# First expert's weight loads tied to all seven routing phases instead of the first one

## The chip, the cores and the metric

The kernel runs on one core of a Trainium2 chip. The metric is the time of one execution on the device, in microseconds (us); lower is better. Five engines work side by side, each through its own list of instructions in order: TensorE (PE: matmuls, and transposes done as matmuls), VectorE (DVE), ScalarE (ACT), GpSimd (POOL) and SyncE (SP, which issues nearly all DMA transfers here).

## What is computed

Three stages, each fed by the one before. Attention over 4 batches of 12 heads (448 tokens, head size 64) with normalised queries and keys; an MLP with an ELU (768 to 2048 to 768) on the 1792 tokens that come out; and a mixture of 8 experts (768 to 1024 to 768) to which the tokens are dealt greedily, at most 224 to an expert:

```python
def _moe_ref(x, w_in, w_out):
    h = x @ w_in
    g = np.where(h > 0.0, h, alpha * (np.exp(np.minimum(h, 0.0)) - 1.0))
    return g @ w_out

def _moe2_ref(x, w_gate, w1, w2):
    cap = N // E
    flat = (x @ w_gate).flatten()
    for idx in np.argsort(-flat):
        tok, e = idx // E, idx % E
        if assigned[tok] >= 0 or counts[e] >= cap:
            continue
        assigned[tok] = e
        counts[e] += 1
    for e in range(E):
        mask = assigned == e
        out[mask] = np.maximum(x[mask] @ w1[e], 0.0) @ w2[e]
```

Matrix products are made of three float16 products each (high part times high, low times high, high times low), so every weight is split on the chip into two float16 tiles.

## The kernel before

**Order of the work.** Up to about 610 us the kernel does attention and the first product of the MLP. From there to about 890 us PE does the MLP's second product (tile `py`, function `second`) and, in between, the routing that deals tokens to experts. After that come the eight experts (`expert`), each with its weights loaded by `load_expert` and its tokens gathered by `gather`. One caller weaves the two: `route_units` gives a number at each `yield` of `Route.phase`, and the loop around it puts as many `py` matmuls into PE's list as that number is worth. So the routing has PE's gaps filled by a fixed list of `py` work, and PE's order is written out by hand.

**A routing phase.** There are seven (`Route.phase(i)`, i = 0 to 6; this text counts them in the same way) and a `finish`. A phase finds each open token's best expert (L91 to L99 on DVE), transposes the scores (PE, `rt_pb`), copies them to `rt_row` (L117), makes 14 comparison tiles `rt_C` on DVE (L127) whose sums PE takes into `rt_pc`, copies these (L138 on ACT, L139 on DVE into `rt_cs`), transposes them on PE (`rt_pg`), and then goes through a chain of small steps that passes between DVE and PE: L151, L152, L154 on DVE, `rt_pm` on PE, L158, `rt_pt` on PE, L162 to L213, `rt_pp` on PE, L175 to L182, `rt_pc` (of `rt_sc`) on PE, L186 to L193, and the next phase's L91. Each PE step of this chain stands in PE's list behind `py` matmuls, and the `py` matmuls behind it wait for it.

`self.marks.append(i)` (L135) notes the last `rt_C` comparison of each phase, so that seven marks exist.

**Loading an expert.** An expert has 14 weight chunks: six of W1 (128 x 1024 float32, 512 KB) and eight of W2 (128 x 768, 384 KB). For each, `load_steps` issues one DMA from SP into a staging tile `st` (L362; three staging buffers, so the fourth load waits until the first chunk is split), and `split` makes the high part on ACT (L350) and the low part on DVE (L351):

```python
st = stg.tile([P, w], F32, tag="st", name="st")
i = nc.sync.dma_start(st, src)
if hold:
    tc.add_manual_dep(i.ins, hold[-1].ins.name, NOSYNC, reason="not before its turn")
split(hi, lo, st, w)
```

`hold[-1]` is what a load is tied to. The tie is of the kind NOSYNC: a scheduler, which places every instruction in the list of its engine by simulated times, may not place the load earlier than the mark. No semaphore comes of it; on the chip SP issues the load when the instructions ahead of it on SP are done and its staging buffer is free. `load_expert(0)` appends the mark of phase 0 to `hold`, and that stays the last entry for all experts.

**Tiles.** Expert 0's weights go to the buffers of pool `wuA`, which are free once the MLP's first product is done (about 611 us). Expert 1's go to `wuB`, which holds `w_out` until the last `py` matmuls. SP also issues the loads of the MLP's middle values (`g`, L790 and L794) and the stores of finished rows `xh` (L817, made by L815 on ACT and L816 on DVE) that the gathers of the experts read.

Of the kernel before, what the change touches and what calls it, by code (L numbers as in the profile page):

```python
# [255 lines left out]
def kernel(  # L256
# [25 lines left out]
    KC = DM // P  # L282
    NF = FF // P
    NF1 = F1 // P
# [61 lines left out]
    hold = []  # L346
# [6 lines left out]
    def load_split(hi, lo, src):  # L353
        for _ in load_steps(hi, lo, src):
            pass

    def load_steps(hi, lo, src):

        w = src.shape[1]
        if src.dtype == F32:  # L360
# [5 lines that stand above are left out]
            yield  # L366
            return

        for a in range(0, w, 512):
            n = min(512, w - a)  # L370
            st = stg.tile([P, n, 2], I32, tag="st", name="st")
            nc.sync.dma_start(st.rearrange("p n t -> p (n t)"), src[:, a:a + n].bitcast(I32))
            cv = gat.tile([P, n], I32, tag="cv", bufs=3, name="cv")
            i = DVE.tensor_scalar(cv, st[:, :, 1], 3, 0x3FFFFFF8, op0=ALU.logical_shift_left, op1=ALU.bitwise_and)
            if pace:
                tc.add_manual_dep(i.ins, pace[-1].ins.name, NOSYNC, reason="not before its turn")
            DVE.scalar_tensor_tensor(cv, st[:, :, 1], -0x40000000, cv, op0=ALU.bitwise_and, op1=ALU.bitwise_or)  # L377
            DVE.scalar_tensor_tensor(cv, st[:, :, 0], 29, cv, op0=ALU.logical_shift_right, op1=ALU.bitwise_or)
            cf = cv.bitcast(F32)
            ACT.activation(cf, cf, AF.Copy, scale=SW)  # L380
            ACT.copy(hi[:, a:a + n], cf)
            POOL.tensor_sub(lo[:, a:a + n], cf, hi[:, a:a + n])
            yield
# [475 lines left out]
    R = Route(nc, mmo, rconst, rsb, psR, dram, NCH, NE, CAP, B, S, id32, id16)  # L859
# [29 lines left out]
    ex = ctx.enter_context(tc.tile_pool(name="ex", bufs=2))  # L889
    KH = KC // 2  # L890

    def load_expert(e):
        if e == 0:
            hold.append(R.marks[0])
        pool = wuB if e % 2 else wuA
        W1 = pool.tile([P, 2, KC, F1], F16, tag="wu", name=f"w1_{e}")
        W2 = pool.tile([P, 2, NF1, DM], F16, tag="wu", name=f"w2_{e}")
        for c in range(KC):
            load_split(W1[:, 0, c, :], W1[:, 1, c, :], w1[e, c * P:(c + 1) * P, :])
        for c in range(NF1):  # L900
            load_split(W2[:, 0, c, :], W2[:, 1, c, :], w2[e, c * P:(c + 1) * P, :])
        return W1, W2

# [18 lines left out]
    def expert(e, W1, W2, xT):  # L922
# [33 lines left out]
        for hh in range(2):  # L956
# [15 lines left out]
            stores.append(st)  # L972

    W, xT = load_expert(0), gather(0)
    for e in range(NE):
        W_, x_ = W, xT
        if e + 1 < NE:
            W, xT = load_expert(e + 1), gather(e + 1)
        expert(e, *W_, x_)
# [30 lines left out]
```

## Time and profile before

| | |
|---|---|
| median of 3 runs | 1160.86 us (1159.09 to 1165.01) |
| the profiled execution | 1164.11 us, its span 1162.4 us |
| PE busy | 1039.3 us, 89% of the span |
| DVE busy | 784.2 us, 67% |
| ACT busy | 539.2 us, 46% |
| mean granted PE clock | 0.963 |

The span runs from the first to the last instruction; the execution's own time is 1.7 us longer. "Busy" is time in which an engine executes; idle time costs only where the chain that ends last goes through it. A timeline row gives start, duration, engine, line, operation and operands, how many instructions were merged into it, and in brackets how long the engine sat idle before it and what ended that. "xN" behind a busy time is a count of instructions.

### The profile page before, as it was taken

The numbers are of one execution on the slowest core, as the hardware profiler recorded it, in microseconds if no ns is written. First come the engines' busy times: TensorE is split into PE (matmuls) and PEld (weight loads), VectorE is DVE, ScalarE is ACT, GpSimd is POOL, SyncE is SP. The second block draws the span as 40 slices with busy tenths as digits, with TensorE's granted clock in tenths as the row PEclk, the third lists the DMA queues.
The fourth block names the chain that finished last, engine by engine and source line by source line (L and its number), as shares of the span: only waits on it lengthen the run. The fifth ranks groups of instructions, "written<-read, shape, count | busy, mean of one in ns | idle before, by whom it ended". The sixth has DMA issues, their size and how long they took to land.

```text
span 1162.4 us, 19353 instructions
## 1 busy us (share of the span) xinstructions
PE 1039.3 (89%) x7030; PEld 608.4 (52%) x7030; DVE 784.2 (67%) x1567; ACT 539.2 (46%) x1099; POOL 353.9 (30%) x462
## 2 busy tenths in 40 slices
PE   0687879897989999999999699999999898999997
PEld 0233334343444445444444345555546687888885
DVE  3788898999988775554337777877775565556520
ACT  2676677776777664554430410011102455555520
POOL 3687775757746451220000000000000412222100
PEclk9888889998999989999999899999999899999999
DMA  6355575569997825336823641030003778778710
GB/s 172 78 133 132 147 207 151 145 178 255 245 256 195 194 68 121 81 95 225 328 55 113 194 167 50 21 130 21 22 21 101 239 236 263 223 244 258 237 47 24
DMA packets 190319, 176.48 MB, mean 152 GB/s; under 512 B 114704, under 2 KB 161808, under 8 KB 189456
## 3 DMA queue, kind: packets, MB, share of 16 engines
q1 hardware_dynamic: 186064, 163.78, 49.5%
q0 software_dynamic: 3328, 11.01, 3.0%
q8 instruction: 55, 0.90, 0.3%
q10 hardware_dynamic: 832, 0.46, 0.1%
q14 instruction: 40, 0.33, 0.1%
HBM read 125.92 MB, written 31.98 MB: 136 GB/s over the span
## 4 chain that ended last, share of the span: by engine, by line
PE 48%; DVE 16%; DMA 13%; issue 10%; ACT 6%; POOL 4%; SPq 2%; POOLq 0%; DVEq 0%; ACTq 0%
PE py L324 17%; PE ph L324 12%; DMA st<-in_moe_w_dram 7%; PE po L324 4%; PE pye L324 3%; PE phe L324 3%; PE ps L324 3%; PE rt_pc L324 2%; DVE w L351 2%; DVE sm L533 2%; ACT w L350 2%; DVE cv L377 2%; PE pta L324 2%; DMA qn<-in_q_dram 2%; PE pl L324 1%
## 5 line engine op out<-in xcount | busy, mean ns | idle before, releaser
L324 PE MATMUL ph<-xT,w_in 128*128 128x448 f16 x1152 | 246.1, 358 | 8.2 <-DVE elu_g L685 5.2
L324 PE MATMUL py<-w_out,g 128*128 128x384 f16 x1152 | 204.5, 329 | 0.0
L324 PEld LDWEIGHTS <-w_in 128*128 128x128 f16 x1152 | 107.7, 99 | 127.7 <-issue 46.1
L351 DVE SCALAR_TENSOR_TENSOR w<-st,w 128x768 f16<-128x768 f32 (+1 forms) x112 | 119.2, 1072 | 76.7 <-ACT w L350 71.5
L545 POOL TENSOR_SCALAR pe<-pe,sm 128x448 f32<-128x448 f32 x168 | 126.7, 764 | 138.8 <-DVE sm L541 70.3
L324 PEld LDWEIGHTS <-g 128*128 128x128 f16 x1152 | 107.4, 98 | 89.3 <-issue 26.7
L324 PE MATMUL ps<-kT,qT 64*128 64x448 f16 (+1 forms) x576 | 97.0, 392 | 56.2 <-ACT pe L535 30.7
L350 ACT ACTIVATE w<-st 128x768 f16<-128x768 f32 (+1 forms) x112 | 103.6, 933 | 90.8 <-DMA st<-in_moe_w_dram 86.5
L535 ACT ACTIVATE pe<-ps,sm 128x448 f32<-128x448 f32 x168 | 105.9, 634 | 50.0 <-DVE sm L533 47.4
L324 PE MATMUL pye<-w,hT 128*112 128x512 f16 (+1 forms) x768 | 126.4, 326 | 0.0
L324 PEld LDWEIGHTS <-w 128*128 128x128 f16 x1152 | 111.8, 100 | 3.3 <-DVE xTe L917 1.2
L127 DVE TENSOR_SCALAR rt_C<-rt_row,rt_m 128x1792 f16<-128x1792 f32 x98 | 107.2, 1149 | 8.2 <-PE rt_pc L324 7.4
L324 PE MATMUL phe<-xTe,w 128*128 128x224 f16 x1080 | 111.4, 264 | 1.1 <-DVE xTe L917 1.1
L533 DVE TENSOR_REDUCE sm<-ps 128x1 f32<-128x448 f32 x168 | 100.2, 615 | 17.2 <-PE ps L324 15.2
L324 PEld LDWEIGHTS <-hT 128*112 128x112 f16 x768 | 91.6, 130 | 32.2
L815 ACT ACTIVATE xh<-py 128x384 f16<-128x384 f32 x28 | 13.7, 491 | 175.0 <-PE py L324 158.1
L324 PEld LDWEIGHTS <-qT 64*128 64x128 f16 (+1 forms) x576 | 27.7, 102 | 99.9 <-issue 66.7
L324 PE MATMUL pta<-id,pe 128*128 128x128 f32 x384 | 64.4, 289 | 15.1 <-POOL pe L545 5.8
L967 POOL DMA_INDIRECT out_dram<-yo,idx x16 | 19.5, 1220 | 179.6 <-DVE yo L966 178.0
L685 DVE SCALAR_TENSOR_TENSOR elu_g<-ph,elu_e 128x448 f32<-128x448 f32 x64 | 39.6, 619 | 48.3 <-ACT elu_e L683 48.1
L324 PEld LDWEIGHTS pta<-id,pe 128*128 128x128 f32 x384 | 45.2, 146 | 44.3 <-POOL pe L545 14.7
L201 POOL MEMSET rt_c<- 128x8 f16 x8 | 0.9, 123 | 220.7 <-DVE rt_c L207 216.6
(176 smaller groups left out, 1470.0 us busy)
## 6 DMA issues: line engine op xcount, KB each, us to landing
st<-in_moe_w_dram SPq DMA_DIRECT2D x48, 512.0 KB
st<-in_moe_w_dram SPq DMA_DIRECT2D x64, 384.0 KB
st<-in_moe_w_in_dram SPq DMA_DIRECT2D x24, 512.0 KB
g_d<-gt SPq DMA_DIRECT2D x64, 192.0 KB
g<-g_d SPq DMA_DIRECT2D x16, 768.0 KB
st<-in_moe_w_out_dram SPq DMA_DIRECT2D x16, 512.0 KB
gl<-g_d SPq DMA_DIRECT2D x32, 192.0 KB
wo_d<-wo SPq DMA_DIRECT2D x16, 384.0 KB
```

The source lines that it names most:

```text
L127: i = DVE.tensor_scalar(C.rearrange("p c t -> p (c t)"), row, m[:, s:s + 1], None, op0=ALU.is_le)
L201: nc.gpsimd.memset(c[:, 0:1, :], 0.0)
L324: i = PE_mm(o, l, r, **kw)
L350: ACT.activation(hi, st, AF.Copy, scale=SW)
L351: DVE.scalar_tensor_tensor(lo, st, SW, hi, op0=ALU.mult, op1=ALU.subtract)
L377: DVE.scalar_tensor_tensor(cv, st[:, :, 1], -0x40000000, cv, op0=ALU.bitwise_and, op1=ALU.bitwise_or)
L533: i = DVE.tensor_reduce(out=st[:, 0, u:u + 1], in_=ps[u], axis=AX.X, op=ALU.max, negate=True)
L535: ACT.activation(p[:, u, :], ps[u], AF.Exp, bias=st[:, 0, u:u + 1], accum_out=st[:, 1, u:u + 1])
L545: POOL.tensor_scalar(p[:, u, :], p[:, u, :], st[:, 2, u:u + 1], 1.0, op0=ALU.mult, op1=ALU.mult)
L685: DVE.scalar_tensor_tensor(gf, ph, -SG / SH, e, op0=ALU.mult, op1=ALU.min)
L815: ACT.activation(xh[:, 0], py, AF.Copy, scale=-SX2 / (SG * SW))
L967: st = POOL.indirect_dma_start(out=out, out_offset=bass.IndirectOffsetOnAxis(ap=idx[:, 1, 2 * e + hh:2 * e + hh + 1], axis=0), in_=yo, in_ ...
```

## The change

`load_expert` no longer appends one mark ahead of all loads. A small function `pace_first` appends, for expert 0 alone, a mark before each chunk: chunk c (0 to 13) gets mark number c * 7 // 14, so chunks 0 and 1 are tied to phase 0, chunks 2 and 3 to phase 1, and so on to chunks 12 and 13 in phase 6. The last entry of `hold`, to which the loads of the other experts are tied, is then the mark of phase 6 instead of phase 0.

```diff
+    def pace_first(e, c):
+
+        if e == 0:
+            hold.append(R.marks[c * len(R.marks) // (KC + NF1)])
+
     def load_expert(e):
-        if e == 0:
-            hold.append(R.marks[0])
         pool = wuB if e % 2 else wuA
         W1 = pool.tile([P, 2, KC, F1], F16, tag="wu", name=f"w1_{e}")
         W2 = pool.tile([P, 2, NF1, DM], F16, tag="wu", name=f"w2_{e}")
         for c in range(KC):
+            pace_first(e, c)
             load_split(W1[:, 0, c, :], W1[:, 1, c, :], w1[e, c * P:(c + 1) * P, :])
         for c in range(NF1):
+            pace_first(e, KC + c)
             load_split(W2[:, 0, c, :], W2[:, 1, c, :], w2[e, c * P:(c + 1) * P, :])
```

The lists of PE and POOL keep their order. On DVE, ACT and SP the splits and loads of expert 0 move. In DVE's list, here the part of phase 0 behind its last `rt_C` (a difference; `w_0_9673` is expert 0's W1, `w_0_9674` its W2):

```order
 L351 SCALAR_TENSOR_TENSOR w_0_9673<-st,w_0_9673 128x1024
 L151 TENSOR_TENSOR rt_w<-rt_pg,rt_rc 128x112
-L351 SCALAR_TENSOR_TENSOR w_0_9673<-st,w_0_9673 128x1024
 L152 SCALAR_TENSOR_TENSOR rt_w<-rt_w,rt_m 128x112
 L154 TENSOR_REDUCE rt_t_7162<-rt_w 128x1
-L351 SCALAR_TENSOR_TENSOR w_0_9673<-st,w_0_9673 128x1024
 L158 TENSOR_REDUCE rt_t_7162<-rt_pm 1x1
-L351 SCALAR_TENSOR_TENSOR w_0_9673<-st,w_0_9673 128x1024
 L162 COPY rt_t_7162<-rt_pt 128x1
 L166 TENSOR_SCALAR rt_ab<-rt_m,rt_t_7162 128x14
 L168 TENSOR_SCALAR rt_at<-rt_m,rt_t_7162 128x14
-L351 SCALAR_TENSOR_TENSOR w_0_9673<-st,w_0_9673 128x1024
```

Of 14 splits that stood between the steps of phase 0's chain, two stay in phase 0, both ahead of L151; the other twelve are gone from it. In DVE's list of phase 1, the part behind its `rt_C` (a difference):

```order
 L816 SCALAR_TENSOR_TENSOR xh<-py,xh 128x384
 L127 TENSOR_SCALAR rt_C<-rt_row,rt_m 128x1792
+L351 SCALAR_TENSOR_TENSOR w_0_9673<-st,w_0_9673 128x1024
 L139 CAST rt_cs<-rt_pc 64x128
 L151 TENSOR_TENSOR rt_w<-rt_pg,rt_rc 128x112
+L351 SCALAR_TENSOR_TENSOR w_0_9673<-st,w_0_9673 128x1024
 L152 SCALAR_TENSOR_TENSOR rt_w<-rt_w,rt_m 128x112
 L154 TENSOR_REDUCE rt_t_7519<-rt_w 128x1
```

Phase 1 has got two splits, one ahead of L139 and one between L151 and L152. In phases 2 to 6 the first stands ahead of L139 too, and the second between L139 and L151; in ACT's list the two L350 of a phase stand on either side of L138. SP's list as it is with the change, from the stores at the start of phase 0 to phase 2 (`st` a staging tile, `x2_d` the finished rows, `g2` and `gt2` the MLP's middle values):

```order
L817 DMA x2_d0_82<-xh_6908 128x768
L362 DMA st_9675<-in_moe2_w1_dram 128x1024
L362 DMA st_9679<-in_moe2_w1_dram 128x1024
L817 DMA x2_d1_83<-xh_7008 128x768
L817 DMA x2_d0_82<-xh_7109 128x768
L790 DMA g2_7535<-g_d2_78 128x3072 x4
L817 DMA x2_d1_83<-xh_7194 128x768
L362 DMA st_9683<-in_moe2_w1_dram 128x1024
L817 DMA x2_d0_82<-xh_7337 128x768
L362 DMA st_9687<-in_moe2_w1_dram 128x1024
L794 DMA gt2_7540<-gt_d1_81 128x4096
L817 DMA x2_d1_83<-xh_7438 128x768
```

Before, all 14 loads of expert 0 and the first three of expert 1 stood ahead of the `g2` load. Now two do, and chunks 2 and 3 stand behind it, each behind a store of `xh`.

## Rows read from the trace of the kernel before

**Rows 1.** Windows: busy time (count) of PE, PEld, DVE, ACT, POOL; clock, DMA share, GB/s.

```profile
621.73:669.46 47.73, 36.21 (x243) 18.84 (x240) 37.81 (x67) 15.77 (x20) 0.13 (x1) 0.93 0.51 162
669.46:703.79 34.33, 33.54 (x240) 18.32 (x241) 26.23 (x60) 3.13 (x6) 0.13 (x1) 1.00 0.44 162
...
644.60:669.46 24.86, 13.90 (x74) 7.28 (x71) 18.52 (x47) 10.68 (x13) 0.13 (x1) 0.86 0.75 231
692.68:703.79 11.11, 11.11 (x72) 6.62 (x71) 7.81 (x37) 0.49 (x1) 0.13 (x1) 1.00 0.35 112
```

**Rows 2.** Timeline of PE in phase 0.

```profile
661.04 0.25 PE L324 MATMUL rt_pp<-rt_c,rt_one 128*128 128x112 f16 x1 [6.61 <-DVE rt_c L213]
661.09 4.04 PE L324 MATMUL py<-w_out,g 128*128 128x384 f16 x12
```

**Rows 3.** Timeline of DVE in phase 0.

```profile
644.07 1.23 DVE L351 SCALAR_TENSOR_TENSOR w<-st,w 128x1024 f16<-128x1024 f32 x1
...
656.20 0.96 DVE L351 SCALAR_TENSOR_TENSOR w<-st,w 128x768 f16<-128x768 f32 x1 [0.81 <-ACT w L350]
...
660.78 0.21 DVE L213 TENSOR_TENSOR rt_c<-rt_c,rt_x 128x112 f16<-128x112 f16 x1
```

**Rows 4.** Timeline of ACT in phase 0: two splits that waited for their loads.

```profile
646.99 1.06 ACT L350 ACTIVATE w<-st 128x1024 f16<-128x1024 f32 x1 [2.00 <-DMA st<-in_moe_w_dram]
649.88 1.06 ACT L350 ACTIVATE w<-st 128x1024 f16<-128x1024 f32 x1 [1.84 <-DMA st<-in_moe_w_dram]
```

**Rows 5.** Timeline of SP: the loads of these two, issued first in each row.

```profile
643.79 1.86 SPq L362 DMA_DIRECT2D st<-in_moe_w_dram  x2
...
645.32 1.65 SPq L362 DMA_DIRECT2D st<-in_moe_w_dram  x2
```

**Rows 6.** Timeline of SP in phases 1 and 4.

```profile
675.35 2.05 SPq L790 DMA_DIRECT2D g<-g_d  x4
677.80 10.34 SPq L817 DMA_DIRECT2D x_d<-xh  x2
...
789.09 10.02 SPq L817 DMA_DIRECT2D x_d<-xh  x2
```

**Rows 7.** Windows, columns as in rows 1: the last transfers of the `g2` load.

```profile
684.00:686.00 2.00, 2.00 (x18) 0.84 (x17) 1.46 (x2) 0.26 (x1) 0.00 (x0) 1.00 0.55 208
```

**Rows 8.** Timeline of DVE in phase 1, around L139 and L151.

```profile
687.71 1.15 DVE L127 TENSOR_SCALAR rt_C<-rt_row,rt_m 128x1792 f16<-128x1792 f32 x1
691.19 0.28 DVE L139 CAST rt_cs<-rt_pc 64x128 f16<-64x128 f32 x1 [2.33 <-ACT rt_cs L138]
693.18 0.28 DVE L151 TENSOR_TENSOR rt_w<-rt_pg,rt_rc 128x112 f32<-128x112 f16 x1 [1.70 <-PE rt_pg L324]
```

**Rows 9.** Timeline of PE in phase 1, around the same steps.

```profile
692.68 0.46 PE L324 MATMUL rt_pg<-id,rt_cs 128*128 128x128 f16 x4
...
694.21 0.27 PE L324 MATMUL rt_pm<-id,rt_t 128*1 128x128 f32 x1
```

**Rows 10.** Timelines of ACT, DVE and PE in phase 2, around the same steps.

```profile
724.67 0.48 ACT L138 CAST rt_cs<-rt_pc 128x384 f16<-128x384 f32 x1 [8.29 <-PE rt_pc L324]
...
726.74 0.56 DVE L816 SCALAR_TENSOR_TENSOR xh<-py,xh 128x384 f16<-128x384 f32 x1 [1.28 <-ACT xh L815]
...
727.82 0.27 DVE L154 TENSOR_REDUCE rt_t<-rt_w 128x1 f32<-128x112 f32 x1
...
728.24 0.27 PE L324 MATMUL rt_pm<-id,rt_t 128*1 128x128 f32 x1
```

**Rows 11.** Timeline of DVE in phase 4.

```profile
793.35 0.28 DVE L139 CAST rt_cs<-rt_pc 64x128 f16<-64x128 f32 x1 [2.17 <-ACT rt_cs L138]
```

**Rows 12.** Windows, columns as in rows 1: short and long idle of PE in phase 0.

```profile
646.00:648.00 2.00, 1.05 (x7) 0.52 (x6) 1.07 (x3) 1.01 (x1) 0.00 (x0) 1.00 0.80 256
...
662.00:664.00 2.00, 2.00 (x8) 0.94 (x7) 1.37 (x4) 1.10 (x2) 0.00 (x0) 0.50 0.84 243
```

**Rows 13.** Timeline of ACT: expert 1's first splits.

```profile
889.71 2.95 ACT L350 ACTIVATE w<-st 128x1024 f16<-128x1024 f32 x3 [3.52 <-PE py L324]
```

## The prediction, made before the changed kernel ran

> **What bounds the kernel now.** I read the windows first, one for each routing phase, because the change touches nothing outside the routing. PE executes nearly all the time there: phase 1 takes 34.33 us, of which PE is busy 33.54, while phase 0 takes 47.73 us for the same list of routing steps and almost the same count of matmuls (243 against 240) [rows 1]. So phase 0 loses time that the other phases do not lose. The windows also tell where: from `rt_pg` to the next phase's `rt_pb` it takes 24.86 us in phase 0 and 11.11 us in phase 1, where PE has no idle time at all [rows 1].
>
> The timeline of PE names the wait. In phase 0 `rt_pp` stood 6.61 us behind the DVE step L213, and twelve `py` matmuls behind it then took 4.04 us [rows 2] at a granted clock of 0.50 [rows 12], which is 1.2 GHz. The timeline of DVE tells why L213 was late: it came at 660.78 us behind splits, and the splits had themselves waited for ACT [rows 3], which had waited for the loads [rows 4]. DVE and ACT go through their lists in order, so a load that is late holds up the small routing steps behind its split. This is a stretch bound by fourteen loads, placed into a chain that PE waits for.
>
> **The change, part by part.** What it removes: twelve of the fourteen splits from phase 0. The most that this can give back is phase 0's excess: 24.86 - 11.11 = 13.75 us by the stretch, 47.73 - 34.33 = 13.40 us by the whole phase [rows 1]. I take 13.6 us. The idle time and the half clock of [rows 2, 12] are inside this figure and are not counted again.
>
> What stays in phase 0: two splits. The second ran from 644.07 for 1.23 us, to 645.30 [rows 3]. In phase 1, L151 begins 0.50 us behind the start of `rt_pg` and `rt_pm` 1.53 us behind it [rows 8, 9]; counted from phase 0's `rt_pg` at 644.60 [rows 1] that is 645.10 and 646.13. L151 is 0.2 us late, so the cost is 0.1 to 0.2 us: 0.15.
>
> What is added to phases 1 to 6: two splits each. The first stands ahead of L139. DVE is free there: in phase 1 the last `rt_C` ends at 688.86 and L139 waits 2.33 us, until 691.19, for ACT [rows 8]. A split of 1.23 us fits, if its load is there. Cost 0 while that idle time covers it; without cover it would delay L139, and PE's `rt_pg` at 692.68 [rows 9] leaves L139's end (691.47) another 1.2 us.
>
> The second split needs ACT after L138, whose end is what L139 waits for. Where the second split stands ahead of L151 (phases 2 to 6), ACT and DVE need 1.06 + 1.23 = 2.3 us for a W1 chunk [rows 3, 4], from 691.19 to 693.5 if phase 1's times are used for the pattern, while L151 begins at 693.18 [rows 8]: 0.3 us late. W2 chunks are three quarters as wide; DVE takes 0.96 us [rows 3], ACT in proportion about 0.8, together under 1.8 us, to 693.0: in time. So phases 3, 4 and 6 cost nothing. In phase 2 the W1 pair has an `xh` step of 0.56 us behind it as well: L138 ends at 725.15, the split at 727.4, then come L151, `xh`, L152 and L154, which ends at about 728.7 instead of 728.09, while `rt_pm` began at 728.24 [rows 10]. Cost 0.5 us. Phase 5 has `xh` ahead of L151 with a W2 split: I put half of that, 0.2 us.
>
> Phase 1 is the exception, since its second split stands between L151 and L152. Nothing covers it: L152 and L154 are 1.23 us later, and `rt_pm`, which ran without idle time and with about 0.1 us to spare, is 1.1 us later.
>
> Are the loads there in time? SP carries them behind stores of `xh` and not behind the marks. In phase 1 chunk 2 stands behind the `g2` load, issued at 675.35 [rows 6], whose transfers ended half way through the window from 684 to 686 [rows 7]. Half a megabyte more at 208 to 256 GB/s [rows 7, 12] is 2.5 us: 687.5, with ACT 688.6, before the last `rt_C` ends. Chunk 3 stands behind the second store of that row, whose issue ended at 688.14 [rows 6]. A load took from 643.79 to 646.99, 3.2 us, when it ran nearly alone, and from 645.32 to 649.88, 4.6 us, among others [rows 4, 5]. So it lands at 691.4 or 692.7, ACT ends by 693.8 at the latest, and DVE wants it at 693.46: nothing, or 0.3 us. In phase 4 the margin is smallest: the store goes out at 789.09, two loads behind it at about 789.4 and 789.8 [rows 6], and L139 stood at 793.35 [rows 11]. With 3.2 us the first is split on ACT by 793.5 and pushes L138 and L139 back 0.6 us, inside the 1.2 us ahead of `rt_pg`; the second split ends 0.2 us behind L151's time. With 4.6 us the phase loses some 1.5 us. I take the 3.2, since phase 4 has no other large transfer: 0.2 us.
>
> Loads of expert 1 are now tied to phase 6. Its first splits waited 3.52 us for `py` [rows 13], that is for its buffer and not for its loads; cost 0. PE's list is the same, so everything from the last `py` on moves forward as a whole.
>
> Sum: 13.6 - 0.15 - 1.1 - 0.5 - 0.2 - 0.2 = 11.4 us. The profiled execution took 1164.11 us and would take 1152.7; it stands 3.25 us above the median of 1160.86, which gives **1149.5 us**. With the low costs (phase 0 0.1, phase 1 1.1, phase 2 0.3, from 13.75) the gain is 12.2; with the high ones (phase 0 0.2, phase 1 1.4, phase 2 0.8, phase 4 1.5, phase 5 0.4, phases 3 and 6 together 0.3, from 13.4) it is 8.8: 1148.7 to 1152.1 us.
>
> PE's clock deserves a sum of its own, as the second-split term makes new idle stretches of up to 1.1 us. Idle time of that size left the clock alone: in the window from 646 to 648 PE was busy only 1.05 of 2.00 us at a granted 1.00, and 0.50 came only behind the 6.61 us [rows 2, 12]. The Trainium skill, "TensorE: Matmul & The Clock Gate", section "A second HAM failure mode: psum-queue depth-cycling", says otherwise of frequent short idle between groups of matmuls: there the clock goes back and forth between its two levels. No run here shows it yet. By the row the sum stays 11.4; what the other would make of it is the third rival.
>
> **The rivals.** *Every phase pays for a split.* If the loads or ACT are a little later than worked out, the second split of every phase lies open, as in phase 1: 3 x 1.23 + 4 x 0.96 = 7.5 us [rows 3], gain 6.1, 1154.8 us. For it: the margins of phases 4 and 5 are a few tenths. Against it: L151 waits 1.70 us for PE [rows 8].
>
> *Slower: the loads come only after the marks.* If SP in effect issues a pair when the last `rt_C` ends, a pair lands 4.6 us later. In phase 1's times: 688.86 + 4.56 = 693.4, ACT and DVE 695.7, L139 to 696.0, where `rt_pg` was to begin at 692.68: 3.3 us, and some 0.5 more for the second. That is 3 x 3.8 + 4 x 3.3 = 24.6 us, against 13.6 won: 11 slower, 1171.9 us. It decides from a loss of 1.9 us in each of seven phases. Against it: the tie gives an order in lists, no wait, and the store ahead of each load is out before the mark.
>
> *The clock drops in each phase.* If each of six phases ran a stretch like that of [rows 2] at half clock, it would lose 2 us each time, 12 in all: gain about 0 to 1, near 1160 us. Against it: [rows 12].
>
> *The gain does not arrive* because something behind the routing ends last in any case. For this I find no row; PE's `py` releases the experts [rows 13].
>
> That the change does not do what it says is excluded by the lists: twelve splits leave phase 0.
>
> **How the numbers follow.** The forecast has 0.72, every phase pays 0.13, the clock 0.04, no arrival 0.07, slower 0.04. About 0.5%, 5.8 us, is what a measurement can tell from no change. The forecast is faster by more, and the first rival lies on that border, so I give it in halves: faster 0.72 + 0.07 = 0.79, same 0.06 + 0.04 + 0.07 = 0.17, slower 0.04. The range takes the forecast's own 1148.7 to 1152.1, 2.7 us below it for the scatter of the runs (1159.09 is 1.8 below their median), and above it the first rival and its scatter: 1146.0 to 1156.5.
>
> **What would show it.** Right: phase 0 from `rt_pb` to `rt_pb` in about 34.3 us, no `rt_pp` wait on L213, the clock at 1.00 through the routing; in phase 1 `rt_pm` waiting about 1.1 us for L154; the other phases between 34 and 35 us. Wrong: ACT's L350 waiting for `st` just ahead of L138 in phase 1 or 4, PE idle over 1 us in more phases than phase 1, a clock below 1.00 behind such a wait, or the gain of the routing given back in the experts.

## The result and the profile after

| | before | changed |
|---|---|---|
| median of 6 runs each, measured together | 1161.69 us (1159.09 to 1165.01) | 1149.4 us (1146.57 to 1154.36) |
| ratio | | 0.9898 (0.9876 to 0.992) |
| the profiled execution | 1164.11 us, span 1162.4 | 1149.89 us, span 1148.2 |
| PE busy | 1039.3 us, 89% | 1037.0 us, 90% |
| mean granted PE clock | 0.963 | 0.968 |

The change makes the kernel 12.3 us (1.0%) faster by the medians; the forecast was 1149.5 us. Windows of the changed kernel, one for each routing phase 0 to 5, cut at the starts of `rt_pb` as in [rows 1] and with the columns of that group:

```profile
623.43:657.82 34.39, 33.83 (x242) 18.58 (x241) 27.77 (x58) 5.02 (x8) 0.13 (x1) 0.99 0.14 49
657.82:692.98 35.16, 33.49 (x242) 18.24 (x240) 27.43 (x58) 5.23 (x8) 0.13 (x1) 1.00 0.46 166
692.98:727.41 34.43, 33.59 (x243) 18.28 (x241) 27.95 (x59) 5.62 (x9) 0.13 (x1) 1.00 0.15 54
727.41:761.56 34.15, 33.48 (x242) 18.24 (x240) 27.73 (x60) 4.59 (x8) 0.13 (x1) 1.00 0.37 133
761.56:795.79 34.23, 33.60 (x244) 18.28 (x241) 26.99 (x59) 4.88 (x9) 0.13 (x1) 1.00 0.12 41
795.79:830.03 34.24, 33.59 (x242) 18.29 (x241) 27.60 (x59) 4.91 (x9) 0.13 (x1) 1.00 0.13 47
```

Phase 0 fell from 47.73 to 34.39 us and PE's clock is 0.99 to 1.00 in all of them. ACT's busy time in phase 0 fell from 15.77 [rows 1] to 5.02 us, and some of it now stands in each of the others: twelve splits have moved. Where PE's idle time went is shown by the waits of PE between 620 and 880 us (in total, how many, the longest). The kernel before:

```profile
PE rt_pp L324 <- DVE rt_c L213: 6.6, 1, 6.6
PE rt_pc L324 <- DVE rt_C L127: 4.3, 7, 0.7
PE rt_pt L324 <- DVE rt_t L158: 1.1, 1, 1.1
PE rt_pb L324 <- DVE rt_m L91: 1.0, 1, 1.0
PE rt_pm L324 <- DVE rt_t L154: 0.9, 1, 0.9
PE rt_pp L324 <- DVE rt_T L172: 0.7, 1, 0.7
PE rt_pc L324 <- DVE rt_sc L182: 0.6, 1, 0.6
```

The changed kernel, the same view:

```profile
PE rt_pc L324 <- DVE rt_C L127: 4.3, 7, 0.7
PE rt_pm L324 <- DVE rt_t L154: 1.3, 2, 1.0
```

The row on `rt_C` is the same in both. The other six of before add up to 10.9 us, and 1.3 us remains: 9.6 us of idle time are gone. In addition PE's busy time in phase 0 fell from 36.21 [rows 1] to 33.83 us, since the stretch at half clock [rows 2, 12] is gone: 2.4 us. Together this is 12.0, and the whole routing, from the first `rt_pb` to the last `rt_pi` (the last PE step of `finish`), takes 252.25 us where it took 264.18: 11.9 us.

The two profiled executions differ by more, 14.2 us. In the changed one the routing began 1.7 us later, and the experts, from their first transposes to the end, took 265.0 us where they took 269.0. The experiments come back to that.

What is left of the splits' cost stands in PE's timeline, phases 0 and 1:

```profile
648.24 0.27 PE L324 MATMUL rt_pm<-id,rt_t 128*1 128x128 f32 x1
...
653.20 0.21 PE L324 MATMUL rt_pp<-rt_c,rt_one 128*128 128x112 f16 x1
...
683.40 0.27 PE L324 MATMUL rt_pm<-id,rt_t 128*1 128x128 f32 x1 [1.00 <-DVE rt_t L154]
```

In phase 0 neither `rt_pm` nor `rt_pp`, which had waited 6.61 us [rows 2], waits any more. In phase 1 `rt_pm` waits 1.00 us, in phase 2 0.27. DVE's timeline in phase 1, from the first split to L154, tells why:

```profile
676.96 1.22 DVE L351 SCALAR_TENSOR_TENSOR w<-st,w 128x1024 f16<-128x1024 f32 x1
679.37 0.28 DVE L139 CAST rt_cs<-rt_pc 64x128 f16<-64x128 f32 x1 [1.19 <-ACT rt_cs L138]
681.36 0.28 DVE L151 TENSOR_TENSOR rt_w<-rt_pg,rt_rc 128x112 f32<-128x112 f16 x1 [1.70 <-PE rt_pg L324]
681.55 1.22 DVE L351 SCALAR_TENSOR_TENSOR w<-st,w 128x1024 f16<-128x1024 f32 x1
...
682.98 0.27 DVE L154 TENSOR_REDUCE rt_t<-rt_w 128x1 f32<-128x112 f32 x1
```

The first split lies inside the idle time ahead of L139: that wait for ACT was 2.33 us [rows 8] and is 1.19 now. The second lies open between L151 and L152, though DVE has 1.70 us of idle time ahead of L151. The place in the order is only part of the reason: ACT ended this chunk's high part at 681.12 (the next rows), so that ahead of L151 at 681.36 the split could have used 0.24 of the 1.70 us. ACT's and SP's timelines show when the loads were there (SP's column is the issue):

```profile
675.22 1.06 ACT L350 ACTIVATE w<-st 128x1024 f16<-128x1024 f32 x1 [0.81 <-DMA st<-in_moe_w_dram]
...
680.06 1.06 ACT L350 ACTIVATE w<-st 128x1024 f16<-128x1024 f32 x1 [0.72 <-DMA st<-in_moe_w_dram]
```

```profile
663.53 1.99 SPq L790 DMA_DIRECT2D g<-g_d  x4
...
666.35 0.44 SPq L362 DMA_DIRECT2D st<-in_moe_w_dram  x1
...
676.37 0.43 SPq L362 DMA_DIRECT2D st<-in_moe_w_dram  x1
```

The load behind `g2` landed by 675.22, 11.7 us behind the issue of `g2` (worked out in the prediction: 12.2). The second landed by 680.06, 3.7 us behind its own issue, between the 3.2 and the 4.6 us of [rows 4, 5]. ACT waits for loads in phases 2 and 5 too (4.34 and 4.02 us), far ahead of L138, where nothing hangs on it. Phase 4 is another matter. ACT's timeline there, and DVE's:

```profile
782.32 0.84 ACT L350 ACTIVATE w<-st 128x768 f16<-128x768 f32 x1 [5.14 <-DMA st<-in_moe_w_dram]
```

```profile
783.19 0.96 DVE L351 SCALAR_TENSOR_TENSOR w<-st,w 128x768 f16<-128x768 f32 x1 [2.41 <-ACT w L350]
784.07 0.28 DVE L139 CAST rt_cs<-rt_pc 64x128 f16<-64x128 f32 x1
```

ACT waited for this load just ahead of L138, which the prediction had named as a sign of being wrong. Counted from the phase's `rt_pb`, L138 is 0.6 us later than before, as forecast, but L139 is 1.1 us later, since the first split stands on DVE ahead of it as well. L139 ends 0.25 us before `rt_pg` (784.60), so PE lost nothing by it; the margin is all but used up.

### The profile page after: what moved, and what is told of

It is laid out like the page before. It is cut to its first block, busy times and chain, and to the rows that moved or that the text cites. A ratio compares the mean times of both kernels' runs of the same rounds, so it can differ in the third digit from the quotient of the medians.

```text
span 1148.2 us, 19348 instructions
## 1 busy us (share of the span) xinstructions
PE 1037.0 (90%) x7030; PEld 608.9 (53%) x7030; DVE 787.0 (69%) x1567; ACT 538.5 (47%) x1099; POOL 354.1 (31%) x462
## 4 chain that ended last, share of the span: by engine, by line
PE 51%; DVE 18%; DMA 11%; issue 10%; ACT 5%; POOL 3%; SPq 2%; POOLq 0%; DVEq 0%; ACTq 0%
PE py L324 18%; PE ph L324 11%; DMA st<-in_moe_w_dram 4%; PE pye L324 4%; PE po L324 4%; PE phe L324 3%; DVE sm L533 2%; PE ps L324 2%; PE rt_pc L324 2%; DVE cv L377 2%; PE pta L324 2%; DMA qn<-in_q_dram 2%; PE pl L324 1%; DVE cv L378 1%; DVE rt_C L127 1%
## 5 line engine op out<-in xcount | busy, mean ns | idle before, releaser
L350 ACT ACTIVATE w<-st 128x768 f16<-128x768 f32 (+1 forms) x112 | 103.8, 933 | 89.3 <-DMA st<-in_moe_w_dram 84.0
L324 PE MATMUL ps<-kT,qT 64*128 64x448 f16 (+1 forms) x576 | 94.3, 382 | 54.5 <-ACT pe L535 29.2
L127 DVE TENSOR_SCALAR rt_C<-rt_row,rt_m 128x1792 f16<-128x1792 f32 x98 | 107.3, 1149 | 8.2 <-PE rt_pc L324 7.4
```

What stands on the lines that cost most here:

```text
L127: i = DVE.tensor_scalar(C.rearrange("p c t -> p (c t)"), row, m[:, s:s + 1], None, op0=ALU.is_le)
L324: i = PE_mm(o, l, r, **kw)
L350: ACT.activation(hi, st, AF.Copy, scale=SW)
```

## The experiments

All phase times below are differences between the starts of `rt_pb` in PE's timeline of one profiled execution; "routing" runs to the last `rt_pi`, "experts" from their first transposes to the end. Phase times repeat closely: phases free of splits take 34.0 to 34.3 us in every kernel.

| kernel | phases 0 to 5, us | routing | experts |
|---|---|---|---|
| before | 47.73, 34.33, 34.03, 34.15, 34.15, 34.15 | 264.18 | 269.0 |
| changed | 34.39, 35.16, 34.43, 34.15, 34.23, 34.24 | 252.25 | 265.0 |
| changed, second time | 34.09, 35.15, 34.43, 34.14, 34.32, 34.24 | 252.01 | 265.1 |
| other experts' tie alone | 47.01, 34.33, 34.02, 34.14, 34.15, 34.15 | 263.44 | 272.0 |
| real wait on the mark | 37.28, 39.69, 38.98, 35.48, 35.96, 35.9 | 270.48 | 265.3 |
| all tied to phase 3 | 34.0, 34.15, 34.03, 36.45, 42.28, 34.15 | 260.71 | 268.1 |
| quarter loads | 48.45, 34.15, 34.02, 34.14, 34.15, 34.15 | 264.70 | 268.8 |
| short low part | 34.12, 37.37, 34.03, 34.14, 34.15, 34.14 | 253.59 | 265.9 |
| copy instead of split | 34.54, 36.66, 34.02, 34.15, 34.15, 34.14 | 253.31 | 268.4 |
| low part on POOL | 42.24, 41.11, 34.02, 34.15, 34.15, 34.15 | 265.47 | 265.9 |
| half at 0, half at 3 | 39.22, 34.15, 34.02, 34.89, 35.53, 34.15 | 257.61 | 265.4 |
| mark one pair earlier | 34.18, 34.14, 34.03, 34.14, 34.15, 34.14 | 250.43 | 268.3 |

**The change a second time.** On another chip, beside the next experiment and "mark one pair earlier".

> The change once more, for its interval and a second profile. My theory of 11.4 us won in the routing: ratio 0.988 to 0.992, phase 0 34.4 us, the whole routing 252 us against 264. The first profile of the change also had 4.0 us less in the experts (265.0 against 269.0 us from the first gathered tile on) and 1.7 us more ahead of the routing, neither of which I had forecast: if they are scatter between executions, the experts lie anywhere from 265 to 269 here; if the change does it, at 265.

Measured: 1155.42 us (1150.03 to 1157.11, 6 runs) against 1167.01 for the kernel before on that chip, ratio 0.9905 (0.9882 to 0.9928). The phases are those of the first profile, phase 0 within 0.3 us and the others within 0.1; the terms of single phases can be read to that.

**The other experts' tie alone.** The change also ties the loads of experts 1 to 7 to phase 6 instead of phase 0. In the kernel before, alone:

```diff
     def load_expert(e):
...
+        if e == 0:
+            hold.append(R.marks[-1])
         return W1, W2
```

> The second effect of the change alone: all loads of expert 0 in phase 0 as before, the other experts' loads tied to the mark of phase 6. The prediction put this at 0: phase 0 47.7 us, routing 264 us, time within 0.3% of before. If this tie is what shortened the experts by 4 us in the change's profile: experts 265 us and ratio 0.996 to 0.998.

Measured: 1169.17 us against 1167.01, ratio 1.0017 (0.9993 to 1.0041); phase 0 takes 47.01 us, the others are those of before. So no effect of this half of the change shows. Its experts took 272.0 us, the longest of all twelve profiles, and the kernel with "mark one pair earlier", which has the same tie, 268.3, while two kernels with the tie of before ("short low part", "low part on POOL") had 265.9. The 4 us by which the experts were shorter in the change's profiles are therefore not put down to this tie. What sets them stays open; the medians (12.3 us) need only the routing's 11.9.

**A real wait on the mark.** The change with a tie that makes SP wait for the mark on the chip:

```diff
-                tc.add_manual_dep(i.ins, hold[-1].ins.name, NOSYNC, reason="not before its turn")
+                tc.add_manual_dep(i.ins, hold[-1].ins.name, SYNC, reason="not before its turn")
```

> The change, but each load waits on the chip for its mark (a semaphore in place of an order for the scheduler). This is the prediction's rival that ends slower. If the tie of the change is only an order, this one must look different: every phase 2.4 to 3.8 us longer than 34.2, in all 17 to 26 us over the change. If the loads of the change already came at their marks: no difference, within 2 us.

Measured: 1173.25 us against 1165.35 (one run each), the routing 18.2 us longer than with the change. The sum is as expected; the single phases lie further apart (1.3 to 5.5 us). In phase 1, from ACT's, DVE's and SP's timelines:

```profile
688.51 1.06 ACT L351 ACTIVATE w<-st 128x1024 f16<-128x1024 f32 x1 [1.47 <-DMA st<-in_moe_w_dram]
```

```profile
689.60 1.23 DVE L352 SCALAR_TENSOR_TENSOR w<-st,w 128x1024 f16<-128x1024 f32 x1 [2.24 <-ACT w L351]
```

```profile
684.77 0.81 SPq L363 DMA_DIRECT2D st<-in_moe_w_dram  x2
```

The pair goes out when the last `rt_C` is done and lands 3.7 us later, and DVE waits 2.24 us for it in the middle of the chain; `rt_pm` then waited for L154 in six phases, 14.0 us in all. This is the slower rival of the prediction made real, with one difference: both splits stand behind L139, so L154 comes late and not L139. It shows what the change is: an order in SP's list, with no wait on the chip.

**All fourteen tied to phase 3.** The kernel before with `R.marks[3]` in place of `R.marks[0]`.

> All fourteen loads tied to the mark of phase 3. My theory: the loss goes with the splits, whatever the phase. Phase 0 takes 34.2 us, and phases 3 and 4 together lose 8 to 14 us; the whole near the kernel before. If phase 0 were special (the MLP's values being loaded beside it, or the end of the first product): no phase loses over 3 us and the time is that of the change.

Measured: 1166.71 us against 1165.35 (one run each). Phase 0 is free (34.0 us), and phases 3 and 4 lose 2.3 and 8.1 us, 10.4 together as expected. The loss goes where the splits go. Its largest piece, from PE's timeline:

```profile
775.84 1.04 PE L324 MATMUL rt_pc<-rt_C,rt_E 128*32 128x512 f16 x8 [4.84 <-DVE rt_E L99]
```

Here another step is late than in phase 0: L99 of phase 4, which makes `rt_E`. Between L91 and L99 the order now has three splits and three `rt_C` comparisons.

**Are late loads the cause, or DVE's own time?** The prediction called phase 0 "a stretch bound by fourteen loads". Three kernels take much of one of the two away. First the loads: the kernel before with a quarter of each load, and the splits as long as before (they read the quarter four times over).

```diff
-            st = stg.tile([P, w], F32, tag="st", name="st")
-            i = nc.sync.dma_start(st, src)
+            m = w // 4 if short else w
+            st = stg.tile([P, m], F32, tag="st", name="st")
+            i = nc.sync.dma_start(st, src[:, 0:m])
+            if short:
+                st = st.unsqueeze(1).broadcast_to([P, 4, m])
+                hi, lo = (x.rearrange("p (r m) -> p r m", r=4) for x in (hi, lo))
```

> All fourteen splits stay in phase 0 and keep their size, but each load of expert 0 brings a quarter of its columns and the split reads them four times over (three quarters of expert 0's weights are left out). My theory: phase 0 lost its time both to late loads and to the splits' own time on DVE. DVE idled 6.3 us in phase 0 for ACT, which waited for loads; that part goes, the splits' own 15 us, of which the chain's idle time covers about half, stay: phase 0 from 47.7 to about 41 us. If late loads alone did it: about 35 us. If the splits' time on DVE alone did it: 47 us or more.

Measured: 1171.78 us against 1165.35 (one run each); phase 0 takes 48.45 us, no less than before. PE's waits, then DVE's (from 620 to 720 us), then the window of phase 0:

```profile
PE rt_pp L324 <- DVE rt_c L213: 4.7, 1, 4.7
...
PE rt_pm L324 <- DVE rt_t L154: 3.6, 1, 3.6
```

```profile
DVE w L351 <- ACT w L350: 2.4, 6, 0.9
```

```profile
629.02:677.47 48.45, 38.40 (x243) 19.75 (x241) 39.12 (x70) 15.65 (x20) 0.10 (x1) 0.89 0.25 78
```

DVE's waits for ACT, and so for loads, are down to 2.4 us in all, where the kernel before had 6.3 in the same view. PE waits all the same, as the splits' own time is in the chain. So the splits' time by itself is enough for a loss of this size, and the 41 us expected were missed. But this is not the kernel before with its waits taken out. The scheduler made another order: three splits stand ahead of L139 and eleven between it and L213, where the kernel before had one and nine (and four behind L213). PE's idle time in phase 0 did fall, from 11.5 us [rows 1] to 10.1; its busy time rose by 2.2 us, from 36.21 to 38.40, as two stretches ran at half clock here (the last section) and one before.

What the loads cost in the order of the kernel before stands in that kernel's own trace. Of nine splits between L139 and L213 four waited for ACT, the fourth by 0.81 us [rows 3], and ACT had waited for their loads [rows 4]:

```profile
648.08 1.23 DVE L351 SCALAR_TENSOR_TENSOR w<-st,w 128x1024 f16<-128x1024 f32 x1 [0.97 <-ACT w L350]
...
650.97 1.23 DVE L351 SCALAR_TENSOR_TENSOR w<-st,w 128x1024 f16<-128x1024 f32 x1 [1.48 <-ACT w L350]
...
658.39 0.96 DVE L351 SCALAR_TENSOR_TENSOR w<-st,w 128x768 f16<-128x768 f32 x1 [0.48 <-ACT w L350]
```

Phase 0 from the start of L139 to that of L213, in DVE's timelines of four kernels (us):

| kernel | L139 to L213 | splits between | their own time | their waits for ACT |
|---|---|---|---|---|
| all tied to phase 3 | 7.12 | 0 | 0 | 0 |
| half at 0, half at 3 | 12.38 | 6 | 7.09 | 1.83 |
| before | 17.10 | 9 | 9.95 | 3.74 |
| quarter loads | 16.52 | 11 | 11.35 | 2.01 |

In each kernel with splits the stretch is longer than 7.12 us by their own time and their waits together, less 3.7 to 4.0 us, which the chain's own idle time covers. By these sums a wait for a load counts here just as a split does. In the kernel before the splits' own time is the larger part; without the waits this stretch would have taken some 13.4 us (an estimate, 17.10 less 3.74), still 6 us more than without splits.

Then the other way, DVE's time taken away and the loads left whole, in two ways. In the first ACT makes seven eighths of each low part with a copy:

```diff
+        if short:
+            m = dst_shape // 8
+            ACT.activation(hi, st, AF.Copy, scale=SW)
+            ACT.copy(lo[:, m:], st[:, m:])
+            DVE.scalar_tensor_tensor(lo[:, 0:m], st[:, 0:m], SW, hi[:, 0:m], op0=ALU.mult, op1=ALU.subtract)
+            return
```

> The kernel before with whole loads, but DVE makes only an eighth of each low part of expert 0 (0.2 us instead of 1.0 to 1.2; ACT writes the rest, so seven eighths of the low parts are left out). The counterpart of the quarter loads, which left phase 0 at 48.5 us and so showed that the splits' time on DVE alone is enough. If that time is the only cause: phase 0 35 to 37 us. If the loads alone are enough too (fourteen at about 2 us each, DVE waiting for ACT, which waits for them): 44 to 48 us, with DVE idle 15 us or more in it.

Measured: 1151.65 us against a median of 1167.01 (one run); phase 0 takes 34.12 us, phase 1 37.37. In the second ACT keeps its work, and DVE copies:

```diff
         ACT.activation(hi, st, AF.Copy, scale=SW)
+        if short:
+            DVE.tensor_copy(lo, hi)
+            return
```

> The kernel before with one edit: VectorE makes the first expert's low part by a copy of the high part instead of the subtraction (the true low part is left out of the computation). The loads, their sizes and ScalarE's high parts stay; VectorE's operation for each piece of 512 columns x 128 should be shorter than the 1.23 us of the split. If phase 0's loss is VectorE's own time for the splits: it shrinks in proportion to that operation's time, and phase 0 takes 34 to 39 us. If the fourteen loads, landing one after the other, are enough to hold the phase up, as the prediction's reason had it: 44 to 48 us as before.

Measured: 1157.09 us against 1168.58 (one run each); 34.54 and 36.66 us. The windows of phases 0 and 1, and one row of DVE's timeline:

```profile
626.09:660.63 34.54, 33.76 (x243) 18.27 (x241) 26.80 (x61) 10.61 (x14) 0.13 (x1) 1.00 0.47 157
660.63:697.29 36.66, 33.66 (x242) 18.45 (x240) 27.57 (x65) 7.75 (x12) 0.13 (x1) 1.00 0.61 215
```

```profile
661.91 0.36 DVE L352 COPY w<-w 128x768 f16<-128x768 f16 x1 [2.04 <-ACT w L350]
```

With pieces of 0.36 to 0.44 us (1024 and 768 columns wide, not 512) instead of 0.96 to 1.23, phase 0 loses 0.5 us. What a late load does by itself is in the last row: a copy ahead of L94 waits 2.04 us for ACT and its load, `rt_C` is late, and phase 1 loses 2.5 us. In the first kernel phase 1's 3.2 us come from ACT: its copies of `rt_row` (L117) stand behind the split operations with their added copies, one of which waited 1.03 us for its load. Each kernel loses some 3 us in phases 0 and 1 together; the loads cost no more than that in these orders, and 44 to 48 us for phase 0 missed by far. But with shorter operations the scheduler made other orders: three and four pieces stand between L139 and L213, where the kernel before had nine splits, and none of them waited for ACT. So neither is the list of before with one duration changed, and what the loads alone would cost in that list is not shown.

**The low part on POOL.** The kernel before, its low parts for expert 0 taken off DVE:

```diff
+        if pool:
+            ACT.activation(st, st, AF.Copy, scale=SW)
+            ACT.copy(hi, st)
+            POOL.tensor_sub(lo, st, hi)
+            return
```

> The kernel before, all loads in phase 0, but expert 0's low parts are made by GpSimd behind ACT, so that no split stands in DVE's list. My theory, that the chain's DVE steps wait behind splits: the wait of rt_pp on L213 goes and phase 0 takes 34 to 38 us, what is left being ACT's copies L117 of phase 1 behind about six loads; routing 9 to 13 us shorter than before. If the transfers themselves or the clock slowed phase 0: 45 us or more, as before.

Measured: 1170.16 us against 1165.35 (one run each); phases 0 and 1 take 42.24 and 41.11 us, and `rt_pp` still waits 5.14 us for L213. This missed all the same, and not for the loads' sake. DVE's and POOL's timelines:

```profile
656.82 2.17 DVE L168 TENSOR_SCALAR rt_at<-rt_m,rt_t 128x14 f32<-128x14 f32 x1
...
660.62 1.99 DVE L206 COPY rt_c<-rt_c 128x64 f16<-128x64 f16 x1
...
662.73 2.11 DVE L213 TENSOR_TENSOR rt_c<-rt_c,rt_x 128x112 f16<-128x112 f16 x1
```

```profile
654.75 4.21 POOL L353 TENSOR_TENSOR w<-st,w 128x1024 f16<-128x1024 f32 x2 [0.69 <-ACT w L352]
...
660.44 4.34 POOL L353 TENSOR_TENSOR w<-st,w 128x1024 f16<-128x1024 f32 x2 [0.23 <-ACT w L352]
```

L213 takes 0.21 us in the kernel before [rows 3] and 2.11 here. The three long DVE operations end at 658.99, 662.61 and 664.84; POOL's splits end at 658.96, at about 662.61 (the middle of the pair) and at 664.78. Each of these three lasts until the POOL split beside it is done. Not every step does: L158 and L162, which read the PSUM tiles `rt_pm` and `rt_pt`, took 0.28 and 0.16 us beside the first of these splits. In phase 1 POOL's splits meet L127 as well: three comparisons take 6.80 us there, and 3.28 in the kernel before. So the run takes the splits out of DVE's list and leaves their time in DVE's chain; it can't tell what the loads alone would cost.

**Half at phase 0, half at phase 3.** The change with `R.marks[3 * (c // 7)]`.

> The change with another table of marks: the first seven pieces tied to the mark of phase 0, the other seven to that of phase 3. If a phase can hide only some of the splits' time on VectorE (two cost about 0 to 1 us in the change, twelve to fourteen cost 13.6 in the kernel before): six or seven splits, about 8 us of VectorE, lose 4 to 7 us in phase 0 and as much in phases 3 and 4 together; the routing takes 258 to 264 us. If a phase has a fixed price for being tied to, whatever the number of pieces: phases 0 and 3 lose 10 or more each, and the routing takes 270 or more. If the loss starts only past some number of pieces above seven: both halves cost under 2 us, and the routing is that of the change, 252 to 254.

Measured: 1157.89 us against 1168.58 (one run each). Seven splits (6 x 1.23 + 0.96 = 8.3 us) cost phase 0 5.1 us, as expected. PE's waits in the routing:

```profile
PE rt_pp L324 <- DVE rt_c L213: 2.5, 1, 2.5
PE rt_pm L324 <- DVE rt_t L154: 1.7, 2, 0.9
PE rt_pt L324 <- DVE rt_t L158: 1.3, 1, 1.3
```

The seven of phase 3 cost only 0.7 + 1.4 = 2.1 us, less than the 4 to 7 expected, and the routing at 257.61 us lies just under the range given. In DVE's list only two of these stand between L139 and L213 (in phase 0 it was six) and one ahead of L139; the other four come behind L213, among L91 to L127 of phase 4, where part of their time lies beside PE work; PE's waits for `rt_C` in the routing grow from 4.3 to 5.4 us. It is not the number of splits in a phase alone that counts, but how many stand between steps that PE waits for.

**The mark one pair of `rt_C` earlier.** If phase 1's 1.0 us comes from the second split behind L151, an earlier mark, which moves the load and the split forward together, should cure it. The change with the mark moved:

```diff
         for s0 in range(0, nch, 2):
...
+            if s0 == nch - 4:
+                self.marks.append(i)
             yield 1.6 if s0 < nch - 2 else 1.7
-        self.marks.append(i)
```

> The change with the mark at the last but one pair of rt_C, which puts both splits of a phase ahead of L139 on DVE. My theory of the cost that was left: in phases 1 and 2 the second split delays L154 by 1.0 and 0.3 us; ahead of L139 DVE idles 2.33 us and rt_pg leaves 1.2 more, so two splits (2.4 us) cost nothing. No rt_pm wait on L154, phases 1 and 2 34.1 to 34.3 us, routing about 251 us, 1.0 to 1.4 us under the change, ratio to before 0.987 to 0.991. Rival: the loads are not there yet when the splits come earlier; then rt_pg waits on L139 and phases 1 and 4 are 1 to 3 us longer.

Measured: 1152.04 us (1150.18 to 1158.66, 6 runs) against 1167.01, ratio 0.9879 (0.9854 to 0.9904). All phases take 34.03 to 34.18 us, the routing 250.43, 1.6 to 1.8 under the change's two profiles, a little more than expected. DVE's timeline in phase 1, and SP's:

```profile
683.97 2.35 DVE L352 SCALAR_TENSOR_TENSOR w<-st,w 128x1024 f16<-128x1024 f32 x2
686.39 0.28 DVE L140 CAST rt_cs<-rt_pc 64x128 f16<-64x128 f32 x1
```

```profile
673.36 1.08 SPq L363 DMA_DIRECT2D st<-in_moe_w_dram  x2
```

Both loads go out at once behind `g2`, the second 10 us earlier in the phase than with the change, and both splits stand ahead of the `rt_cs` copy (L139, here L140), whose 2.33 us of waiting [rows 8] they fill to the last tenth. By the phases this is the best version: the splits of the first expert now cost nothing that the phases show. By the whole time it can't be told from the change (the intervals overlap); by the phases it can.

## Why the prediction was right, and where its reason falls short

- **Phase 0.** Forecast 13.6 - 0.15 = 13.45 us, measured 47.73 - 34.39 = 13.3, and 13.6 by the second profile. Right.
- **Phase 1.** Forecast 1.1 us from the split between L151 and L152; PE waited 1.00 us there, and the phase grew by 0.83. Right. The last experiment, which moves this split and its load together, takes the cost away; it does not tell the place from the load's time.
- **Phases 2, 4, 5.** Forecast 0.5, 0.2 and 0.2; measured 0.40, 0.08 and 0.09. Right in size. In phase 4 the delay of L139 was mis-sized, 1.1 us for 0.6, and still inside the gap ahead of `rt_pg`. Phase 3 costs nothing in either.
- **The loads.** The arrivals were worked out to within the bounds of the rows; in phase 4 the first load was there 3.3 us behind its issue (3.2 taken).
- **Sum.** 11.4 us forecast for the routing, 11.9 measured. That the median came out within 0.1 us of the forecast is luck beyond this: by the medians the gain was 12.3, 0.9 more than forecast, and the median of before was 1161.69, 0.8 more than the 1160.86 that the forecast started from. The runs of one kernel spread over 8 us.
- **The other experts.** Their first splits waited 3.52 us for `py`, as before [rows 13], and their tie alone showed no effect. Right.

ACT's timeline of the changed kernel, expert 1's first splits:

```profile
879.48 2.95 ACT L350 ACTIVATE w<-st 128x1024 f16<-128x1024 f32 x3 [3.52 <-PE py L324]
```

**The reason falls short** in the sentence "This is a stretch bound by fourteen loads". The prediction read the waits of ACT for `st` [rows 4] as the cause since they came first in the chain, and gave no weight to the splits' own time. Both stand in the chain: between L139 and L213 nine splits of 9.95 us and 3.74 us of waits. With loads a quarter as large the loss stayed, in an order with eleven splits there; with DVE's pieces a third as long, and three or four of them there, some 3 us were left in two phases. So in the list that the scheduler makes with early loads phase 0 loses as much, and in the list of before the splits' own time is the larger part; how the 13.6 us divide in the list of the kernel before is known from its trace alone, as no kernel changed one of the two and kept the list. It did not harm the number, because moving the splits takes both away.

**The rivals.** That every phase pays for a split (1154.8 us) fell: only phase 1 shows an open one, and phase 2 pays 0.4 us. The slower rival, loads that come only after the marks, did not happen, and the kernel that forces it has a routing 20.1 us longer than the one in which no split lies open (250.43), where the prediction had 24.6: the phases with W1 chunks lost 3.1 to 5.5 us each (3.8 taken), those with W2 chunks 1.3 to 1.8 (3.3 taken). The clock rival fell too: it stays at 1.00 behind phase 1's wait. For the Trainium skill, "TensorE: Matmul & The Clock Gate", section "A second HAM failure mode: psum-queue depth-cycling", this means that no going back and forth shows here.

## What to carry to other kernels

Where a chain of small steps passes between two engines, bulk work placed between its steps on an in-order engine costs its own duration and its waits for data, less what the chain's own gaps cover (3.7 to 4.0 us here), so it can cost much even when its data are early. Ask first where that engine waits for something else, and give each such gap as much bulk work as it holds (here 2.3 us behind the last comparison, two splits). A wait at the head of a late chain is not yet its whole cause: add up the work and the waits in the chain, and look at the order again after every edit, since a scheduler may make another list. A tie in the scheduler's order adds no wait on the chip, while the same tie as a real wait turned a gain of 12 us in the routing into a loss of 6.

## What the runs showed of the hardware

**POOL holds up DVE.** Beside a POOL split of some 2.1 us, three DVE steps that take about 0.2 us alone took 2.0 to 2.2 and ended with it (the rows of "the low part on POOL"). The Trainium skill, "SBUF — State Buffer", section "SBUF: two separate sides", states that VectorE and GpSimd share a pair of ports which one of them takes for a whole instruction while the other is blocked; on VectorE's side this holds for a two-port mode or two inputs in SBUF. These rows agree, and so do L158 and L162, which read from PSUM and were not held up. Moving the splits from DVE to POOL did not free DVE's chain here.

**Idle time and PE's clock.** Phase 0 of "half at 0, half at 3" kept a granted clock of 1.00, though `rt_pp` waited 2.5 us in it:

```profile
625.59:664.81 39.22, 33.89 (x243) 18.32 (x241) 33.06 (x63) 9.87 (x13) 0.13 (x1) 1.00 0.32 107
```

With quarter loads, where `rt_pm` waited 3.6 us and `rt_pp` 4.7, the clock was 0.50 afterwards both times (two windows of that kernel):

```profile
660.00:662.00 2.00, 2.00 (x8) 0.96 (x7) 1.69 (x3) 1.41 (x2) 0.00 (x0) 0.50 0.29 75
670.00:672.00 2.00, 1.97 (x8) 0.93 (x8) 1.60 (x8) 0.00 (x0) 0.00 (x0) 0.50 1.01 311
```

So shrinking a wait can give back more than the wait: in phase 0 of the kernel before it was 2.4 us of slow matmuls on top of the idle time.
